# A conditioned decode block: filler matmuls taken out behind the last P.V, four small loads put on another queue, load semaphores shared

## The chip, the cores and the metric

The kernel runs on one core of a Trainium2 chip. The time is the device time of one execution in microseconds (us); before the change it is 665.49, the median of 3 runs (665.31 to 665.92).

## The reference

A decode step for 4 sequences of one token each, in bfloat16: layer norm with conditioned scale and shift, attention over a cache of 4096 positions and 32 heads of width 128, then a gated MLP with its own norm. Cut to what matters:

```python
mod = (silu(c) @ w_mod).reshape(4, 6, 1, 512)      # w_mod 512 x 3072
sa, ca, ga, sb, cb, gb = mod[:, 0], ..., mod[:, 5]
h = layernorm(x) * (1 + ca) + sa
q = (h @ wq) as (B=4, H=32, 1, 128)                # wq 512 x 4096
p = softmax(q . k_cache * 128 ** -0.5)             # k_cache, v_cache: 4 x 32 x 4096 x 128
x = x + ga * ((p . v_cache) as (4, 1, 4096) @ wo)  # wo 4096 x 512
h = layernorm(x) * (1 + cb) + sb
z = gelu(h @ w_in)                                 # w_in 512 x 1792, z1 | z2 of 896 each
g = w_sp * layernorm(z2) + b_sp                    # one token: w_sp and b_sp are scalars
x = x + gb * ((z1 * g) @ w_out)                    # w_out 896 x 512
```

The two caches together are 268 MB and are read once; everything else is some 14 MB.

## The kernel before

**Order and waits.** Every instruction is entered in program order into a list for its engine (`Program.add`, L54). From the tiles that it reads and writes, `Program.depend` (L75) works out which earlier instructions of other engines it must follow, and `Program.order` (L110) which of these need a wait. A wait is for a semaphore that the awaited instruction or load counts up: a load adds 16 to the semaphore that it was given by name (`Program.load`, L164), an instruction 1 to one for its engine and its reader. An engine works through its list strictly in order. The instructions of PE, DVE and ACT that belong to the 15 looped heads stand in a hardware loop of 5 passes with 3 head groups in each; SP, which issues the loads, has them written out. The profile gives DVE and ACT instructions the line of the common helper (L160), matmuls those of `mm` (L382) or `moving` (L392), explicit weight loads L387, and loads L166; so they are told apart by their tiles and their time.

**The front (L410 to L539).** ACT issues four small loads: the 4 rows of c and the 4 rows of x into the tile `rows`, and the scalars w_sp and b_sp into `wb_t`. SP issues w_mod (`wm`, 3 MB), wq (4 MB), then the first K and V (8 MB each). All scratch of the front, `wm`, `wq` and `rows` too, lies in the third of three 8 MB buffers `kv`. PE transposes c and x (eight small matmuls, L506 and L509), ACT and DVE make silu(c), `ln_stats` (L463) makes the mean and the inverse deviation of x by a matmul with a constant matrix, and `mod_part` (L481) makes one of the six modulation vectors with 16 matmuls of 4 columns each; the first two parts read `wm` with a stride of 4 columns. `query` (L493) multiplies by `wq`, once for each sequence, and ACT copies the queries to `qbc`.

**The attention (L624 to L643).** One step is a group of 8 heads of one sequence: 16 steps, of which the last stands outside the loop. In a step, K (8 MB) arrives in one of the three buffers and V in the next. `scores` (L546) multiplies a quarter of K by the query on DVE (the products with 8192 elements for each partition) and adds up over the width on PE with the identity as weights, 16 matmuls of 512 columns; `fold` and `softmax` follow on DVE and ACT; `values` (L594) multiplies by V on PE; `diagonal` (L607) and `project` (L614) pick each head's part and divide by the sum, in the following step. The next K is issued once `diagonal` has freed its buffer (V of the step before).

**The tail (L646 to L770).** Behind the last V, SP issues the late loads into the third buffer (L652 to L656): Wo in three pieces (`GS`), w_in in two (`WJS`), w_out in two (`JFS`); the last four wait until all of V has landed (`v_done`). Each of the seven has a semaphore of its own, `any_late0` to `any_late6`. On PE stand, in order: the last `values`, `sums`, `diagonal` and `project`; `permute` (L661), which puts the heads in the order in which Wo's rows arrive; `output` (L672), 64, 48 and 16 pairs of a weight load and a 4-column matmul (`mm2`, L401), one call for each piece of Wo; the second norm with its statistics matmul; 56 pairs with w_in; two gelus on ACT, with the table for gelu loaded before them (L717) and that for exp and log after (L739); the third norm; 28 pairs with w_out; and a transpose of the result `yo` (L764), a copy and the store.

`busy(n)` (L681) puts fillers between these: it loads the identity as weights and issues n matmuls of 512 columns of `qbc` into a PSUM bank that nobody reads. It is called with 13 before the last P.V and with 2, 2, 5, 2, 2, 7 and 4 behind it.

Of the kernel before, what the change touches and what calls it, by code (L numbers as in the profile page):

```python
# [252 lines left out]
def kernel(  # L253
# [18 lines left out]
    B, _, D = A_x.shape  # L272
    _, H, SK, DH = A_k_cache.shape
# [22 lines left out]
    wb_t = sb.tile([1, 2], BF16, name="wb_t")  # L296
    ident = sb.tile([P, P], BF16, name="ident")
# [19 lines left out]
    qbc = sb.tile([P, NQ, DH], BF16, name="qbc")  # L317
# [10 lines left out]
    def parts(t, a, *ns):  # L328
        for n in ns:
            yield t[:, a:a + n]  # L330
            a += n


    wm, wq, hbc, rows, ones_b, xb, xcT, sg, hn = parts(
        kv[2], 0, J * 6 * D, J * H * DH, J * B * 64, D, P, *(2 * n * J * B for n in (2, 2, 1, 1)),
    )
# [4 lines left out]
    rows, ones_b = rows[0:2 * B], ones_b[0:1]  # L341
# [8 lines left out]
    attn_b, small, po_b, zo_b, s_b = *banks[0:4], banks[4:8]  # L350

    def cut(t, *dims):
        n = 1
        for d in dims:
            n *= d
        t = t[:, 0:n]
        if len(dims) == 1:
            return t
        names = "abcd"[:len(dims)]
        return t.rearrange(  # L360
            f"p ({' '.join(names)}) -> p {' '.join(names)}", **dict(zip(names[1:], dims[1:]))
        )
# [6 lines left out]
    prog = Program(nc, ("PE", "DVE", "ACT"))  # L369

    def dve(name, *args, **kw):
        return prog.call("DVE", name, *args, **kw)
# [13 lines left out]
    def weights(lhsT):  # L386
        prog.add("PE", lambda e, it: e.ldweights(lhsT), [lhsT], [], done=False)  # L387

    def moving(out, lhsT, rhs, start, stop, done=False, sem=None):

        def emit(e, it):
            return e.add_instruction(mybir.InstMatmult(  # L392
                name=nc.get_next_instruction_name(), engine=mybir.EngineType.PE,
                ins=[e.lower_ap(rhs), e.lower_ap(lhsT, for_matmul_weights=True)],
                outs=[e.lower_ap(out)], start_tensor_calc=start, stop_tensor_calc=stop,
                tile_size=(P, P), tile_position=(0, 0), ldweights=False,
                bass_skip_group_check=True,
            ))
        prog.add("PE", emit, [rhs], [out], done=done or sem is not None, sem=sem)
# [7 lines left out]
        return col[:, None, :].to_broadcast([P, n, B])  # L407


    prog.load("ACT", "any_rows_c", rows[0:B], c)  # L410
    prog.load("ACT", "any_rows_x", rows[B:2 * B], A_x.rearrange("b s d -> (b s) d"))
    prog.load("ACT", "any_wb_w", wb_t[:, 0:1], B_w_sp[0:1, 0:1])
    prog.load("ACT", "any_wb_b", wb_t[:, 1:2], B_b_sp.rearrange("(a b) -> a b", b=1))
    tables = "natural_log_exp_and_others"
    prog.add("ACT", lambda e, it: e.preload_act_table_set(tables), [], [], done=False)

    prog.load("SP", "any_wm", wm, w_mod.rearrange("(p j) n -> p (j n)", j=J))
    prog.load("SP", "any_wq", wq, A_wq.rearrange("(p j) n -> p (j n)", j=J))
    wm = wm.rearrange("p (j n) -> p j n", j=J)
    wq = wq.rearrange("p (j g h d) -> p j g h d", j=J, g=G, h=NH)  # L420
# [18 lines left out]
    def load_v(i):  # L439
        n = 2 if i == NQ - 1 else 1  # L440
        w = NT * DH // n
        for a in range(n):
            last = prog.load(
                "SP", f"any_v{a}" if i == NQ - 1 else f"pe_v{i % NB}",
                buf(2 * i + 1)[:, a * w:(a + 1) * w], kv_view(A_v_cache, i)[:, a * w:(a + 1) * w],
            )
        return last
# [143 lines left out]
    def sums():  # L591
        mm(z_ps, mean_d, rsh, True, True, sem="sp")
# [14 lines left out]
    def diagonal():  # L607
        for n in range(4):
            mm(
                o_ps, osb[:, n, :], sel[:, NH * n:NH * n + NH],  # L610
                n == 0, n == 3, sem=("sp", None, None, "dve")[n],
            )

    def project(i):  # L614
        dve("reciprocal", out=rz, in_=z_ps, sem="dve")
        if i >= NQ - 2:
            o = dict(out=oT[:, i + 1])
        else:
            k = (i + 1) % NB
            ov = oT[:, 0:NP * NB].rearrange("p (g k) h -> p g k h", k=NB)  # L620
            o = dict(dyn=lambda g: {"out": ov[:, g, k]})
        dve("tensor_tensor", in0=o_ps, in1=rz, op=MULT, sem="pe", **o)

    load_k(0)  # L624
    for i in range(NQ):
        prog.passno = i // NB if i < NQ - 1 else None
        v_done = load_v(i)
# [23 lines left out]
    GS = [(0, 4), (4, 7), (7, 8)]  # L651
    late = [(wo[:, a:b], wo_v[:, a:b]) for a, b in GS]  # L652
    late += [(win[:, a:b], win_v[:, a:b]) for a, b in WJS]
    late += [(wout[:, a:b], B_w_out[a * P:b * P].rearrange("(p j) n -> p j n", p=P)) for a, b in JFS]
    for n, (t, src) in enumerate(late):
        prog.load("SP", f"any_late{n}", t, src, after=[v_done] if n > 2 else ())  # L656

    oP = oP.rearrange("p (g r b) -> p g r b", g=8, r=4)
    heads = oT[:, 1:].rearrange("p (g b) (e h) -> p h g e b", b=B, e=2)
# [1 line left out]
    def permute(a, b):  # L661
        pp = cut(s_b[2], b - a, 4, B)
        for r in range(4):
            for hl in range(4):
                mm(
                    pp[hl * 32:(hl + 1) * 32, :, r, :], ident[:, r::4],
                    heads[:, hl, a // 2:b // 2], True, True, r == hl == 3,
                    tile_position=(0, hl * 32),
                )
        dve("tensor_copy", out=oP[:, a:b], in_=pp)  # L670

    def output(a, b):  # L672
        for g in range(a, b):
            for r in range(4):
                for jo in range(J):
                    mm2(
                        attn_ps[:, jo, :], wo[:, g, r, jo * P:(jo + 1) * P], oP[:, g, r, :],
                        g == r == jo == 0, g == 7 and r == 3, g == 7 and r == jo == 3,
                    )

    def busy(n, bank=s_b[3]):  # L681

        weights(ident)
        for _ in range(n):
            moving(cut(bank, 4, DH), ident, qbc[:, 0:4, :], True, True)

    busy(13, attn_b)
    permute(0, 6)
    pool("memset", mean_f, 1.0 / FH)
    values(NQ - 1)  # L690
    sums()
    busy(2)
    diagonal()
    project(NQ - 1)
    busy(2)
    permute(6, 8)
    for (a, b), n in zip(GS, (5, 2, 2)):
        output(a, b)
        busy(n)


    x1 = x1b[:, 0]
# [9 lines left out]
    h = h.rearrange("p (j b) -> p j b", b=B)  # L712
    dve("tensor_tensor", out=h, in0=xs, in1=modT[:, 3], op=ADD)

    busy(7)
    gelu = "gelu_apprx_tanh_and_others"
    prog.add("ACT", lambda e, it: e.preload_act_table_set(gelu), [], [], done=False)  # L717
    zp = {1: cut(s_b[0], JF, B), 0: cut(s_b[1], JF, B)}
# [40 lines left out]
    dve("tensor_tensor", out=q, in0=q, in1=bc(rstd, J), op=MULT)  # L759
    yo = yo.rearrange("p (b j) -> p b j", b=B)  # L760
    dve("tensor_tensor", out=yo.rearrange("p b j -> p j b"), in0=q, in1=r1, op=ADD)
    busy(4)
    t_ps = small[0:J * B, 0:P]
    mm(t_ps, yo.rearrange("p b j -> p (b j)"), ident, True, True, True)  # L764
    ot = ot[0:J * B]
# [47 lines left out]
```

## Time and profile before

| | |
|---|---|
| median of 3 runs | 665.49 us (665.31 to 665.92) |
| the profiled execution | 665.31 us, span 663.5 us, mean granted TensorE clock 0.80 |
| busy, share of the span | PE 403.0 us (61%), DVE 391.3 us (59%), ACT 27.3 us, POOL 2.7 us |
| moved | 282.73 MB read, 426 GB/s over the span |
| filler matmuls | 37, 12.3 us busy |
| load from issue to landing | w_mod 10.2 us, wq 20.2 us, the late loads 13.7 to 26.2 us |
| store of the result | 1.4 us from issue to landing |

The span runs from the first to the last instruction; the profiled execution's time has 1.8 us around it. Times inside the span are given as us from its start. A row in order of time reads: start, duration, engine, line, operation, written tile, read tiles, shape, number of merged instructions, and in brackets the engine's idle time before it with what ended that. PEld are weight loads, which overlap with matmuls. A row of merged instructions gives the stretch that they cover. The granted clock is a share of TensorE's full clock.

### The profile page before, as it was taken

What the parts mean: (1) busy time and instruction counts of PE and PEld (TensorE: products, weight loads), DVE (VectorE), ACT (ScalarE), POOL (GpSimd) and SP (SyncE); (2) the same over time, 40 slices, a digit from 0 to 9 for tenths busy, and PEclk for the clock granted to TensorE, in tenths of its full rate; (3) what the DMA queues carried; (4) which work ended last, traced back from release to release, by engine and by line L of the source; (5) the groups of instructions that cost most, each with busy time, mean ns of one, the idle gap of its engine ahead of it and who ended that gap; (6) DMA issues with size and microseconds to landing.
All of it is one profiled execution on the core that took longest, in us unless ns stands there. A gap on an engine that the chain in (4) does not pass through costs nothing.

```text
span 663.5 us, 5137 instructions
## 1 busy us (share of the span) xinstructions
PE 403.0 (61%) x2738; PEld 79.3 (12%) x1749; DVE 391.3 (59%) x331; ACT 27.3 (4%) x64; POOL 2.7 (0%) x11
## 2 busy tenths in 40 slices
PE   2527485563748456374846637494663749466787
PEld 2200101010010101001010100101010010101123
DVE  2058292855829285582928558292855829286942
ACT  1100000000000000000000000000000000000002
POOL 1000000000000000000000000000000000000000
PEclk9959687686968768696876869687686968768996
DMA  9999999999999999999999999999999999999995
GB/s 372 452 435 442 416 431 427 440 435 435 439 431 419 439 442 435 439 431 442 423 423 442 439 435 442 427 431 427 435 442 439 431 435 435 427 427 429 440 407 222
DMA packets 7148, 282.86 MB, mean 426 GB/s; under 512 B 732, under 2 KB 740, under 8 KB 2532
## 3 DMA queue, kind: packets, MB, share of 16 engines
q1 hardware_dynamic: 7120, 282.73, 98.7%
q8 instruction: 7, 0.11, 0.1%
q10 hardware_dynamic: 20, 0.01, 0.0%
q14 instruction: 1, 0.01, 0.0%
HBM read 282.73 MB, written 0.00 MB: 426 GB/s over the span
## 4 chain that ended last, share of the span: by engine, by line
DMA 65%; PE 23%; DVE 11%; issue 0%; SPq 0%; ACT 0%
DMA kv<-in_A_k_cache_dram 58%; PE bank L392 22%; DVE kv L160 11%; DMA kv<-in_A_wo_dram 4%; DMA kv<-in_A_wq_dram 3%; PE bank L382 2%; SPq L166 0%; ACT kv L160 0%; SPq L808 0%; SPq L772 0%
## 5 line engine op out<-in xcount | busy, mean ns | idle before, releaser
L160 DVE TENSOR_TENSOR kv<-kv,qbc 128x8192 bf16<-128x8192 bf16 x64 | 280.3, 4420 | 188.9 <-DMA kv<-in_A_k_cache_dram 188.9
L392 PE MATMUL bank<-kv,ident 128*128 128x512 bf16 x1024 | 261.4, 418 | 159.1 <-DVE kv L160 158.9
L382 PE MATMUL bank<-kv,Ph 128*32 128x512 bf16 x1024 | 88.9, 523 | 1.0 <-DMA kv<-in_A_v_cache_dram 1.0
L160 DVE TENSOR_REDUCE S<-bank 128x64 f32<-128x512 f32 x64 | 43.9, 686 | 36.9 <-PE bank L392 36.9
L382 PE MATMUL bank<-rsh,mean_d 128*128 128x8 f32 x32 | 9.3, 364 | 79.0 <-DVE rsh L160 79.0
L387 PEld LDWEIGHTS <-ident 128*128 128x128 bf16 x72 | 8.7, 121 | 300.4 <-issue 300.4
L160 DVE TENSOR_TENSOR Ph<-E,mask 128x2048 bf16<-128x2048 f32 (+1 forms) x19 | 36.9, 1955 | 10.7 <-ACT E L160 10.7
L382 PEld LDWEIGHTS bank<-kv,Ph 128*32 128x32 bf16 x1024 | 32.9, 127 | 49.5 <-issue 40.7
L160 ACT ACTIVATE E<-S,nm 128x256 f32<-128x256 f32 x16 | 8.1, 508 | 455.1 <-DVE nm L160 455.1
L382 PEld LDWEIGHTS bank<-rsh,mean_d 128*128 128x128 f32 x32 | 7.8, 303 | 140.4 <-DVE rsh L160 140.0
L382 PEld LDWEIGHTS bank<-sel,osb 128*128 128x128 f32 x136 | 17.8, 192 | 55.4 <-issue 54.6
L382 PE MATMUL bank<-sel,osb 128*128 128x8 f32 x136 | 16.3, 247 | 0.0
L160 ACT COPY osb<-bank 128x512 f32<-128x512 f32 x16 | 9.4, 586 | 137.4 <-PE bank L382 137.4
L392 PE MATMUL bank<-qbc,ident 128*128 128x512 bf16 x37 | 12.3, 473 | 0.0
L382 PE MATMUL bank<-kv 128*32 128x512 bf16 x129 | 9.4, 460 | 4.5 <-DMA kv<-in_A_wq_dram 4.5
L387 PEld LDWEIGHTS <-kv 128*128 128x128 bf16 x212 | 6.5, 104 | 5.2 <-DMA kv<-in_A_wo_dram 3.0
L160 DVE TENSOR_REDUCE mx<-S 128x1 f32<-128x256 f32 x16 | 6.7, 420 | 0.5
L392 PE MATMUL bank<-kv,kv 128*128 128x4 bf16 (+1 forms) x212 | 6.5, 168 | 0.6 <-DMA kv<-in_A_wo_dram 0.3
L160 DVE RECIPROCAL rz<-bank 128x8 f32<-128x8 f32 x17 | 3.4, 201 | 4.8 <-PE bank L382 4.8
L382 PE MATMUL bank<-ident,kv 8*128 8x8 bf16 (+2 forms) x9 | 0.6, 176 | 8.4 <-DMA kv<-in_A_x_dram 8.4
L382 PE MATMUL bank<-sT,kv 128*128 128x4 bf16 x96 | 3.7, 169 | 2.4 <-DVE modT L160 1.8
L382 PEld LDWEIGHTS bank<-kv 128*32 128x32 bf16 x129 | 3.9, 114 | 10.0 <-DMA kv<-in_A_wq_dram 4.6
(76 smaller groups left out, 51.4 us busy)
## 6 DMA issues: line engine op xcount, KB each, us to landing
kv<-in_A_k_cache_dram SPq DMA_DIRECT2D x2, 4096.0 KB, 18.9
kv<-in_A_v_cache_dram SPq DMA_DIRECT2D x2, 4096.0 KB, 31.5
kv<-in_A_wq_dram SPq DMA_DIRECT2D x1, 4096.0 KB, 20.2
kv<-in_w_mod_dram SPq DMA_DIRECT2D x1, 3072.0 KB, 10.2
kv<-in_A_wo_dram SPq DMA_DIRECT2D x1, 2048.0 KB, 21.5
kv<-in_A_wo_dram SPq DMA_DIRECT2D x1, 1536.0 KB, 24.8
kv<-in_B_w_in_dram SPq DMA_DIRECT2D x1, 1344.0 KB, 13.7
kv<-in_A_wo_dram SPq DMA_DIRECT2D x1, 512.0 KB, 26.2
```

The lines of the kernel that those rows point to most:

```text
L160: return getattr(e, name)(*args, **kw, **(dyn(it) if dyn else {}))
L382: "PE", lambda e, it: e.matmul(out, lhsT=lhsT, rhs=rhs, start=start, stop=stop, **kw),
L387: prog.add("PE", lambda e, it: e.ldweights(lhsT), [lhsT], [], done=False)
L392: return e.add_instruction(mybir.InstMatmult(name=nc.get_next_instruction_name(), engine=mybir.EngineType.PE, ins=[e.lower_ap(rhs), e.lowe ...
```

## The change

Three things are done.

- The helper `busy` goes, and with it all its calls but the first. The first, 13 matmuls into the bank of the attention's output, is written out in its place. Behind the last P.V, 24 filler matmuls and 7 loads of the identity are gone; the order of the other instructions stays.
- The four small loads (c, x, w_sp, b_sp) are issued by SP in place of ACT, behind w_mod and ahead of wq. ACT's first instruction is now the load of its table.
- The seven late loads count on the semaphores of the loads of w_mod, wq, c, x, the two scalars and the first half of the last K, in place of seven of their own. An early load brings such a semaphore to 16, the late one to 32.

```diff
-    prog.load("ACT", "any_rows_c", rows[0:B], c)
-    prog.load("ACT", "any_rows_x", rows[B:2 * B], A_x.rearrange("b s d -> (b s) d"))
-    prog.load("ACT", "any_wb_w", wb_t[:, 0:1], B_w_sp[0:1, 0:1])
-    prog.load("ACT", "any_wb_b", wb_t[:, 1:2], B_b_sp.rearrange("(a b) -> a b", b=1))
     tables = "natural_log_exp_and_others"
     prog.add("ACT", lambda e, it: e.preload_act_table_set(tables), [], [], done=False)
 
     prog.load("SP", "any_wm", wm, w_mod.rearrange("(p j) n -> p (j n)", j=J))
+    prog.load("SP", "any_c", rows[0:B], c)
+    prog.load("SP", "any_x", rows[B:2 * B], A_x.rearrange("b s d -> (b s) d"))
+    prog.load("SP", "any_w", wb_t[:, 0:1], B_w_sp[0:1, 0:1])
+    prog.load("SP", "any_b", wb_t[:, 1:2], B_b_sp.rearrange("(a b) -> a b", b=1))
     prog.load("SP", "any_wq", wq, A_wq.rearrange("(p j) n -> p (j n)", j=J))
...
+    early = ["any_wm", "any_wq", "any_c", "any_x", "any_w", "any_b", "any_k0"]
     for n, (t, src) in enumerate(late):
-        prog.load("SP", f"any_late{n}", t, src, after=[v_done] if n > 2 else ())
+        prog.load("SP", early[n], t, src, after=[v_done] if n > 2 else ())
...
-    def busy(n, bank=s_b[3]):
-
-        weights(ident)
-        for _ in range(n):
-            moving(cut(bank, 4, DH), ident, qbc[:, 0:4, :], True, True)
-
-    busy(13, attn_b)
+
+    weights(ident)
+    for _ in range(13):
+        moving(cut(attn_b, 4, DH), ident, qbc[:, 0:4, :], True, True)
     permute(0, 6)
     pool("memset", mean_f, 1.0 / FH)
     values(NQ - 1)
     sums()
-    busy(2)
     diagonal()
     project(NQ - 1)
-    busy(2)
     permute(6, 8)
-    for (a, b), n in zip(GS, (5, 2, 2)):
+    for a, b in GS:
         output(a, b)
-        busy(n)
...
-    busy(7)
     gelu = "gelu_apprx_tanh_and_others"
...
     dve("tensor_tensor", out=yo.rearrange("p b j -> p j b"), in0=q, in1=r1, op=ADD)
-    busy(4)
     t_ps = small[0:J * B, 0:P]
     mm(t_ps, yo.rearrange("p b j -> p (b j)"), ident, True, True, True)
```

## The prediction

> **What bounds the kernel.** I read the page's queue table and chain first, then the stages, then the first 42 us and the last 15 us in order of time.
>
> ```profile
> q1 hardware_dynamic: 7120, 282.73, 98.7%
> ...
> DMA 65%; PE 23%; DVE 11%; issue 0%; SPq 0%; ACT 0%
> ```
>
> One load queue holds the 16 DMA engines for 98.7% of the span, and transfers are 65% of the chain that ended last. The stages (us, then busy time and count of PE, PEld, DVE, ACT, POOL; the last three columns are the granted TensorE clock, the DMA share and GB/s):
>
> ```profile
> 60.00:600.00 540.00, 325.26 (x1926) 55.23 (x1091) 332.76 (x236) 16.62 (x42) 0.00 (x0) 0.79 1.00 434
> ...
> 646.00:648.00 2.00, 2.00 (x51) 1.11 (x45) 0.00 (x0) 0.00 (x0) 0.00 (x0) 0.85 1.03 422
> ...
> 652.00:654.00 2.00, 2.00 (x7) 0.53 (x3) 1.19 (x9) 0.20 (x1) 0.00 (x0) 0.50 1.02 416
> 654.00:656.00 2.00, 2.00 (x36) 1.01 (x31) 0.41 (x3) 1.59 (x3) 0.00 (x0) 0.94 0.80 319
> ```
>
> Through the loop the DMA share is 1.00 at 434 GB/s, so the loop runs at the rate of the loads. The clock in the tail is half (0.50) although PE is filled all the time, and comes up again only for the stretch from 654. Now the front, in order of time:
>
> ```profile
> 8.42 0.37 PE L382 MATMUL bank<-ident,kv 8*128 8x8 bf16 x8 [8.42 <-DMA kv<-in_A_x_dram]
> ...
> 12.17 0.70 PE L382 MATMUL bank<-sT,kv 128*128 128x4 bf16 x16 [0.27 <-DVE modT L160]
> ...
> 14.46 0.59 PE L382 MATMUL bank<-sT,kv 128*128 128x4 bf16 x16 [0.74 <-DVE modT L160]
> ...
> 17.45 0.37 DVE L160 TENSOR_SCALAR gwb<-modT,wbf 128x16 f32<-128x16 f32 x2
> 21.68 8.64 PE L382 MATMUL bank<-kv 128*32 128x512 bf16 x116 [4.47 <-DMA kv<-in_A_wq_dram]
> ...
> 41.24 4.42 DVE L160 TENSOR_TENSOR kv<-kv,qbc 128x8192 bf16<-128x8192 bf16 x1 [23.42 <-DMA kv<-in_A_k_cache_dram]
> ```
>
> The work that hangs on c and x runs from 8.42 to 17.82, then PE idles until wq lands and starts the queries at 21.68; the loop's first product waits for K at 41.24. And the tail:
>
> ```profile
> 649.11 1.44 PE L392 MATMUL bank<-kv,kv 128*128 128x4 bf16 x48
> ...
> 651.06 0.68 PEld L387 LDWEIGHTS <-kv 128*128 128x128 bf16 x16 [0.57 <-DMA kv<-in_A_wo_dram]
> 651.21 0.61 PE L392 MATMUL bank<-kv,kv 128*128 128x4 bf16 x16
> ...
> 652.96 2.30 PE L392 MATMUL bank<-qbc,ident 128*128 128x512 bf16 x7
> ...
> 654.66 0.17 DVE L160 TENSOR_TENSOR kv<-xs,modT 128x16 bf16<-128x16 f32 x1
> ...
> 655.10 1.83 PE L392 MATMUL bank<-kv,kv 128*128 128x4 bf16 x56
> ...
> 656.97 0.22 ACT L160 ACTIVATE kv<-bank 128x56 bf16<-128x56 f32 x1 [0.36 <-PE bank L392]
> ...
> 657.20 1.28 ACT L739 ACT_TABLE_LOAD   x1
> ...
> 658.19 1.87 PE L392 MATMUL bank<-qbc,ident 128*128 128x512 bf16 x4
> ...
> 659.34 0.21 DVE L160 TENSOR_TENSOR kv<-q,r 128x16 bf16<-128x16 f32 x1
> ...
> 659.99 0.09 PEld L382 LDWEIGHTS bank<-ident,kv 128*16 128x16 bf16 x1 [1.72 <-DVE kv L160]
> ```
>
> Here the chain is on PE, and fillers (the rows bank<-qbc,ident) stand in it.
>
> **The fillers, place by place.** 24 matmuls and 7 loads of the identity go; the 13 at 633.8 stay. What counts is how long a filler makes PE late for work that was ready.
> - Two at 642.71 (0.22 us each at the full clock): done near 643.15; the next work waits for the copy of osb until 643.18. Nothing.
> - Two at 644.14: done at 644.57; oT is ready at 644.73. Nothing.
> - Five at 647.04: 0.22 us until the clock halves, then 0.43; done near 648.8; the second piece of Wo arrives at about 649.06. Nothing, and every slower matmul before 649 hides behind that arrival too.
> - Two at 650.41: PE reaches the last 16 pairs at 651.21, while their weights were there at 651.02 and the weight load stood at 651.06. 0.14 us late.
> - Two at 651.69: done at 652.49; the squares are ready at 652.45, and the usual gap from DVE to PE is 0.05. Nothing.
> - Seven from 652.96: the 56 pairs with w_in start at 655.10; h is ready at 654.66 + 0.17 = 654.83, so 654.88 was possible (the weights landed at 640.51 + 13.7 = 654.2). 0.22 us late.
> - Four from 658.19: the transpose starts at 659.99; yo is ready at 659.34 + 0.21 = 659.55, so 659.60 was possible. 0.39 us late.
>
> So without fillers the w_in pairs start 0.14 + 0.22 = 0.36 us earlier.
>
> **What the clock takes back.** The seven fillers brought the clock up at 654.2; without them I expect 0.50 to the end. Price of a pair (weight load and 4-column matmul): at full clock 64 of them with Wo take 645.42 to 647.04, 25.3 ns; at half 48 take 649.11 to 650.41, 27.1 ns. The w_in pairs read weights with a stride: (1.83 - 0.17)/55 = 30.2 ns at mostly full clock (0.17: the last one's latency). Strided pairs at half are in the front: in the query stage a group of four 512-column matmuls takes 0.43 us up to 26.27 and 0.21 after it, so PE was at half there before the profile's first clock record (the 1.00 it shows is no record). There 16 strided ones take 0.70 and 16 plain ones 0.59, thus (0.70 - 0.17)/15 = 35 and 28 ns. I take 34 ns for w_in: 55 x (34 - 30.2) = 0.21. Bounds: 0 (the clock comes up anyway), and 55 x 30.2 = 1.66 (every pair doubles); 34 lies by the rows nearest in shape.
> [...]
>
> The second gelu (656.97) thus moves by -0.36 + 0.21 = -0.15. Behind it stand the table load (657.20 to 658.48), Ln, Exp (to 659.03) and the two products up to yo: all -0.15, yo at 659.40. The fp32 statistics matmul of the last norm slows from 0.43 us towards the 0.64 us of the half-clocked one at 652.51; its variance is then ready near 658.1, before the table load ends at 658.33, which hides it. The y pairs wait for wout's second piece, landing near 657.7 (642.70 + 15.0); 12 pairs later is 658.2, no later than now. That landing is what is late next: more than about 0.2 us of further gain on the gelu side would stop at it. The transpose then starts at 659.45 instead of 659.99: **-0.54 us** at the end.
>
> **c, x and the two scalars on the load queue.** Four issues leave ACT (0.56 + 0.26 + 0.27 + 0.27 us there) and stand on SP ahead of wq, K and V: SP's own issues take 0.39 to 0.56, so wq is issued at about 3 instead of 1.39, with K and V behind it. Cover: wm, in flight until 0.94 + 10.2 = 11.1. Without it the queue would idle some 1.6 us. ACT's table load, now at 2.40, comes first; its first user is at 8.72. New wait: c and x land behind wm, near 11.3 in place of 8.3. Queued behind on PE: the eight transposes, the norm, all six modulation parts, and the queries; ACT's exp and the DVE chain follow them. All of it moves by 3.0, ending near 20.8. PE still waits for wq at 21.68, 0.9 us later: 0 on the path. With that cover gone the queries would be late, but the loop's product has qbc by 31.6 and K only at 41.24, another 9.6 us. On the queue, the same four transfers use the same 16 engines as before. Bound: seven transfers in line in the tail (642 to 654) ran at 419 against 434 GB/s, 12 x 15/434 = 0.41 us for about six boundaries, so four cost at most 0.3; from below, 0. I take 0.
>
> **Semaphores.** The late loads count to 32 on semaphores whose first 16 were reached long before (the last, K's first half, landed by 611.3; its partner is issued at 642.7). Same waits, another constant: 0; what hides it is that nothing early is still waiting there.
>
> **Code.** 31 PE instructions less may shift a code fetch: the queue for instructions holds 0.6% of 16 x 20 us between 640 and 660 for two fetches, 0.96 us of one engine each, and the last piece waits for the slowest engine. Taken as 0, bounds -0.6 and +0.6.
>
> Sum: 665.31 - 0.54 = 664.77 for the profiled execution (span 663.5, 1.8 around it). The median is 0.18 above it: **664.95**.
>
> **Rivals.**
> - *The clock turns it (slower).* Place: the 56 and 28 pairs after 654. If halving doubles a pair, the w_in stretch ends at 654.74 + 3.5 = 658.24, 1.31 late; u is ready near 658.8, 28 pairs at 54 ns end near 660.4, and yo comes at 661.3: the transpose 1.36 late, 666.85. It decides once a strided pair costs above about 44 ns (55 x 14 = 0.75 eats 0.36 + 0.39). For: the tail's clock follows the filling. Against: 27.1 beside 25.3 ns.
> - *Small transfers hold their ring (slower).* The output, 4 KB alone, takes 1.4 us from issue to landing; if each of four held the lowest engines so long ahead of wq, their share of every later load ends up to 5.6 late: 670.5. It decides from 0.14 us each. Against: 419 GB/s in the tail.
> - *A code fetch leaves the last loads (faster).* Wo's and w_in's last pieces come up to 0.6 earlier: 664.35, or 663.9 with the clock's upper bound.
> - *The removal does nothing.* The fillers' delays are the shadow of the loads' arrivals: 665.5. Against: yo ready 0.39 us before its reader.
>
> **How the numbers follow.** Forecast 0.60; nothing 0.08; code fetch 0.12; clock 0.11; ring 0.06; something unseen 0.03. By 0.2% (1.33 us, about what a measurement of this kernel tells from no change), slower is the ring, half of the clock case and a little unseen: 0.13. Faster needs 664.16 or less: over half of the code fetch and the edge of the forecast: 0.15. Between them 0.72. The forecast's own range, 664.5 to 665.5, widens downwards by the code fetch to 664.0 and upwards towards the clock case to 666.3.
>
> **What would show it.** Right: the first PE work near 11.3 and the queries still at 21.7; clock 0.50 from 647 to the end; 56 w_in pairs from about 654.75 in some 2.05 us; the transpose 0.05 us after yo; last loads landing within 0.3 us of now. Wrong: w_in pairs over 44 ns, wq or K landing later, a loop above 38.6 us for each head group's K and V, or last loads shifted by more than half a microsecond.

## The result, and the profile after

| | before | after |
|---|---|---|
| median | 665.67 us (12 runs, 665.18 to 666.61) | 664.12 us (12 runs, 663.62 to 665.49) |
| ratio | | 0.9977, 95% interval 0.9968 to 0.9986 |
| profiled execution, span | 665.31, 663.5 | 664.01, 662.1 |

So the kernel is 1.55 us faster by the medians, 0.1 to 0.3% by the interval; 0.54 us had been forecast (664.95). The queue and the chain, from the page after:

```profile
q1 hardware_dynamic: 7140, 282.74, 98.9%
...
DMA 60%; PE 22%; DVE 14%; another core or an unknown queue 2%; issue 1%; ACT 0%; SPq 0%; DVEq 0%
```

The load queue still fills the span, now with the four small loads in it (20 packets more), and the loop still runs at 434 GB/s (60 to 598). Transfers are 60% of the chain in place of 65%; among the rest is one step of 12.19 us from 67.87 that the profile could not assign. The front in order of time (start, duration, engine, line, operation, tiles, count, idle time before):

```profile
11.33 0.37 PE L382 MATMUL bank<-ident,kv 8*128 8x8 bf16 x8 [11.33 <-DMA kv<-in_A_x_dram]
...
20.11 0.37 DVE L160 TENSOR_SCALAR gwb<-modT,wbf 128x16 f32<-128x16 f32 x2
...
20.62 9.35 PE L382 MATMUL bank<-kv 128*32 128x512 bf16 x129 [0.75 <-DMA kv<-in_A_wq_dram]
```

The work on c and x begins 2.91 us later, as SP's order makes it, and ends at 20.48 (20.11 + 0.37), just before wq lets the queries start. The cover was thinner than it had looked: wq landed 1.06 us earlier than in the profile before, so this chain ended 0.14 us ahead of the queries where 0.9 had been counted. Its last rows are not read by the queries; PE itself had been free for 0.75 us (the bracket of the third row), against 4.47 before. It was enough. Now the tail:

```profile
649.21 1.89 PE L392 MATMUL bank<-kv,kv 128*128 128x4 bf16 x64 [1.85 <-DMA kv<-in_A_wo_dram]
651.13 0.17 DVE L160 TENSOR_TENSOR x1b<-bank,modT 128x16 f32<-128x16 f32 x1 [5.70 <-PE bank L392]
...
653.92 0.18 DVE L160 TENSOR_TENSOR kv<-xs,modT 128x16 bf16<-128x16 f32 x1
654.15 1.86 PE L392 MATMUL bank<-kv,kv 128*128 128x4 bf16 x56 [1.74 <-DVE kv L160]
...
656.05 0.22 ACT L160 ACTIVATE kv<-bank 128x56 bf16<-128x56 f32 x1 [0.37 <-PE bank L392]
...
658.42 0.21 DVE L160 TENSOR_TENSOR kv<-q,r 128x16 bf16<-128x16 f32 x1
658.69 0.09 PEld L382 LDWEIGHTS bank<-ident,kv 128*16 128x16 bf16 x1 [1.27 <-DVE kv L160]
```

The reader is to see three things. Wo's second and third pieces are now one unbroken stretch of 64 pairs, where two fillers had parted 48 from 16. The w_in pairs start 0.05 us after h is ready (653.92 + 0.18), and the transpose 0.06 us after yo. And the clock stays down (us, busy time and count of PE, PEld, DVE, ACT, POOL, then granted clock, DMA share, GB/s):

```profile
652.00:654.00 2.00, 0.42 (x2) 0.39 (x3) 1.02 (x7) 0.88 (x3) 0.00 (x0) 0.50 1.04 422
654.00:656.00 2.00, 1.85 (x57) 1.82 (x56) 0.29 (x2) 1.10 (x2) 0.00 (x0) 0.50 0.81 325
```

The 56 w_in pairs take 1.86 us at half clock, against 1.83 at full clock before.

Step by step, profile against profile: the product behind Wo moves from 651.86 to 651.13 (-0.73), h by -0.74, the w_in pairs from 655.10 to 654.15 (-0.95), the second gelu from 656.97 to 656.05 (-0.92), yo from 659.34 to 658.42 (-0.92), the transpose from 659.99 to 658.69 (-1.30), which is the whole difference of the two profiled executions. Two steps fit the forecast (0.22 at the seven, 0.39 at the four); two don't: 0.73 in place of 0.14 at Wo, and 0.03 in place of 0.21 given back to the clock.

Wo's last piece also landed earlier, and that made a second suspect. By the semaphore counts of the trace it came 1.96 us after the second piece before (651.02 and 649.06), and 1.30 after the change (650.46 and 649.16). So 0.56 of the 0.73 us at Wo is the piece itself being there sooner; the later pieces came earlier with it (w_out's second at 656.97 in place of 657.71).

### The profile page after: what moved, and what is told of

The parts are those of the page before. It is cut to its first block, busy times and chain, and to the rows that moved or that the text cites. A ratio compares the mean times of both kernels' runs of the same rounds, so it can differ in the third digit from the quotient of the medians.

```text
span 662.1 us, 5106 instructions
## 1 busy us (share of the span) xinstructions
PE 395.1 (60%) x2714; PEld 79.2 (12%) x1742; DVE 391.3 (59%) x331; ACT 27.3 (4%) x64; POOL 2.7 (0%) x11
## 4 chain that ended last, share of the span: by engine, by line
DMA 60%; PE 22%; DVE 14%; another core or an unknown queue 2%; issue 1%; ACT 0%; SPq 0%; DVEq 0%
DMA kv<-in_A_k_cache_dram 56%; PE bank L392 21%; DVE kv L160 13%; DMA kv<-in_A_wo_dram 4%; PE bank L382 0%; SPq L166 0%; DVE S L160 0%; ACT L733 0%; ACT rstd_ln L160 0%; ACT E L160 0%; DVE x1b L160 0%; DVE mx L160 0%; DVE rsh L160 0%; DVE nm L160 0%
## 5 line engine op out<-in xcount | busy, mean ns | idle before, releaser
L160 DVE TENSOR_TENSOR Ph<-E,mask 128x2048 bf16<-128x2048 f32 (+1 forms) x19 | 36.9, 1955 | 10.7 <-ACT E L160 10.7
```

Of the source, the lines that this page charges most:

```text
L160: return getattr(e, name)(*args, **kw, **(dyn(it) if dyn else {}))
```

## The experiments

All are told against `before` run beside them on the same chip. Ratios are with their 95% interval.

**e1: the fillers alone.** As in the change, `busy` and its calls but the first go; loads and semaphores stay.

```diff
-        busy(n)
...
-    busy(7)
...
-    busy(4)
```

> Only the 24 fillers behind the last P.V are taken out; the small loads stay with ACT and the late loads keep their own semaphores. Theory A (the fillers' delays count 0.14 + 0.22 + 0.39 = 0.75 us, and the other 0.6 us of the gain is earlier landings of the last loads that come with the shorter PE code): the whole gain, 1.3 to 1.6 us below before, Wo's last piece landing near 650.5. Theory B (the 0.6 us of landings comes with the four small loads on SP): 0.7 to 0.8 us below before, the last piece of Wo still near 651.0. Theory C (the 0.6 us is the chance of one execution): 0.7 to 0.8 us in the median, landings scattered.

Measured: 664.10 against 665.58, ratio 0.9978 (0.9967 to 0.9988). The whole gain is the fillers'. Wo's last piece landed 1.29 us after the second.

**e2: the small loads alone.**

```diff
-    prog.load("ACT", "any_rows_c", rows[0:B], c)
...
+    prog.load("SP", "any_c", rows[0:B], c)
```

> Only the four small loads move to SP behind w_mod; fillers and semaphores as before. Theory A: no change in the time (0.1 us either way), last landings as before. Theory B: the last loads land about 0.6 us earlier; the fillers hide part of that (PE is full up to 651.2 and up to 655.1), so 0.2 to 0.6 us below before. The forecast's own term: 0, first PE work near 11.3, queries not later than before.

Measured: 665.78 against 665.58, ratio 1.0001 (0.9992 to 1.0010): no change, as the forecast had it. Theory B falls: here the last piece landed late again, 2.09 us after the second. The tail of this profile held the finding that the later runs followed up:

```profile
652.85 3.17 PE L392 MATMUL bank<-qbc,ident 128*128 128x512 bf16 x7
...
654.55 0.17 DVE L160 TENSOR_TENSOR kv<-xs,modT 128x16 bf16<-128x16 f32 x1
655.81 1.88 PE L392 MATMUL bank<-kv,kv 128*128 128x4 bf16 x56
...
660.37 0.27 PE L382 MATMUL bank<-ident,kv 128*16 128x128 bf16 x1 [0.41 <-DVE kv L160]
```

The PE program is that of before, yet the w_in pairs start 1.09 us after h (654.72), and the transpose 0.05 after yo (660.11 + 0.21). The stages of the same profile show where the clock stood:

```profile
654.00:656.00 2.00, 2.00 (x10) 0.34 (x6) 0.35 (x2) 1.49 (x2) 0.00 (x0) 0.50 0.70 279
656.00:658.00 2.00, 2.00 (x59) 1.92 (x56) 0.21 (x2) 0.45 (x3) 0.00 (x0) 0.90 0.06 25
```

Here the clock came up at about 656.4, behind the seven fillers, so that all of them ran at 0.43 us; before, it came up at 654.2, among them. The same rise is then still there for the four ahead of the transpose, which end in time.

**e3: the semaphores alone.**

```diff
+    early = ["any_wm", "any_wq", "any_rows_c", "any_rows_x", "any_wb_w", "any_wb_b", "any_k0"]
...
-        prog.load("SP", f"any_late{n}", t, src, after=[v_done] if n > 2 else ())
+        prog.load("SP", early[n], t, src, after=[v_done] if n > 2 else ())
```

> Only the late loads count on semaphores of early loads. All theories: no change, within 0.1 us of before. Its profile is a further look at how far the last landings scatter without any change of the work.

Measured: 665.28 against 665.58, ratio 0.9996 (0.9987 to 1.0005). No change that can be told. In its profile the last piece landed 1.87 us after the second.

**e4: only the 13 fillers that stood ahead of ready work.**

```diff
-    for (a, b), n in zip(GS, (5, 2, 2)):
+    for (a, b), n in zip(GS, (5, 0, 2)):
         output(a, b)
-        busy(n)
+        if n:
+            busy(n)
...
-    busy(7)
...
-    busy(4)
```

> Only the fillers that stood ahead of ready work are taken out (2 behind the second piece of Wo, 7 ahead of w_in, 4 ahead of the transpose), 13 of 24; the other 11 stay. By the forecast's place-by-place reading these carry the whole 0.75 us: the same time as with all 24 out (e1), to 0.15 us. If the clock in the tail mattered, the kept ones would make it faster than e1. Rival: the gain goes with the number of instructions, so about 13/24 of e1's.

Measured: 664.12 against 665.58, ratio 0.9975 (0.9965 to 0.9986): the time of e1. Thirteen fillers carry all of it, and which of them lay on the path had been read rightly. What taking them out gains had not: 1.46 by the medians, not 0.75.

**e5: each filler replaced by a load of the identity.** No filler's product was used by anything.

```diff
         for _ in range(n):
-            moving(cut(bank, 4, DH), ident, qbc[:, 0:4, :], True, True)
+            if bank is attn_b:
+                moving(cut(bank, 4, DH), ident, qbc[:, 0:4, :], True, True)
+            else:
+                weights(ident)
```

> Each of the 24 fillers behind the last P.V is replaced, in its place, by one more load of the identity as weights (some 0.05 us each, against 0.22 to 0.43 for a filler): the PE program is as long as before and laid out as before, but the fillers' delays are gone, to 0.1 us. Theory A (the earlier landings come with the shorter PE program, which moves a code fetch to another load engine): Wo's last piece lands 1.9 to 2.1 us after the second, as with the fillers, and the time is 0.75 to 0.95 us below before, 0.5 to 0.7 above e1. Theory D (the fillers' own work on PE holds the last loads back): the piece lands 1.3 us after the second, as in e1, and the time is that of e1, some 1.5 below before. Theory E (the fillers' delays were mis-sized, the landings are a side show): the time of e1 whatever the landings.

Measured: 664.23 against 665.86, ratio 0.9974 (0.9965 to 0.9983), and the last piece 1.29 us after the second. From its profile:

```profile
649.44 2.01 PE L392 MATMUL bank<-kv,kv 128*128 128x4 bf16 x64 [1.89 <-DMA kv<-in_A_wo_dram]
...
652.36 0.62 PEld L387 LDWEIGHTS <-ident 128*128 128x128 bf16 x8
...
654.27 0.17 DVE L160 TENSOR_TENSOR kv<-xs,modT 128x16 bf16<-128x16 f32 x1
654.50 1.86 PE L392 MATMUL bank<-kv,kv 128*128 128x4 bf16 x56 [1.74 <-DVE kv L160]
```

The program is as long as before and the gain is there in full: the length and layout of the PE program are not its cause, and theory A falls. What is gone is the time that fillers held PE. The early landing came along in this run too, so it does not part theory D from theory E.

**e6: fillers out, PE's code padded in the front.** The 31 loads write nothing.

```diff
+    for _ in range(31):
+        weights(ident)
     for b in range(B):
```

> The fillers are out as in e1, and 31 loads of the identity are put in the front ahead of the queries, where PE waits for wq: the PE program has its old length, with nothing added to the tail. Theory A by length: the landings as before (1.9 to 2.1 us from Wo's second to its last piece), 0.5 to 0.7 us above e1. Theory A by place in the tail, D and E: landings and time of e1, 1.5 us below before. None expects a change in the front, since the loads there wait for nothing that PE does.

Measured: 664.24 against 665.86, ratio 0.9975 (0.9964 to 0.9985), the last piece 1.49 us after the second. The time of e1 again.

**e7: the other 13 fillers out, those ahead of the last P.V.**

```diff
-    busy(13, attn_b)
```

> The other way about: the 24 fillers behind the last P.V stay, and the 13 ahead of it go (14 PE instructions). Theory A: Wo's last piece lands 1.3 us after the second, as without the fillers, and PE, held by its two fillers, gains at most 0.3 us from that; the clock may halve earlier, which slows the last P.V by up to 1.5 us behind the arrival of Wo (none on the path). Theory D: 1.9 to 2.1 us, as before. For the seven fillers ahead of w_in this is a further look: they end 0.1 to 1.1 us after h is ready, by where the clock comes up.

Measured: 665.47 against 665.86, ratio 0.9993 (0.9984 to 1.0003): no change that can be told. Here the last piece landed early, 1.31 us after the second, with the 24 fillers in place, so theory D doesn't hold as a rule, and nothing was gained by the landing: the two fillers held PE, and the 16 pairs started 2.06 us after the 48. The seven held the w_in pairs by 1.05 us.

**e8 and e9: the gain in two halves.** e8 takes out only the two between Wo's pieces, e9 only the seven and the four.

```diff
 # e8
-    for (a, b), n in zip(GS, (5, 2, 2)):
+    for (a, b), n in zip(GS, (5, 0, 2)):
 # e9
-    busy(7)
-    busy(4)
```

> Only the two fillers between Wo's second and last piece go; 22 stay. Forecast's sizes: 0.14 us below before. Revised theory (the two hold the last 16 pairs to some 2.1 us after the start of the 48; without them PE follows the landing at some 1.3 us): the 16 pairs start 1.3 to 1.4 us after the start of the 48 and the time is 0.6 to 0.75 us below before, less or more by where the clock comes up among the seven.

> Only the seven ahead of w_in and the four ahead of the transpose go; the two stay. Forecast's sizes: 0.61 us below before, less the clock's 0.21, so 0.4. Revised theory: 0.5 to 1.05 us by where the clock would have come up, less 0.03 for the slower clock, so some 0.8 us below before; e8 and e9 together make up e4's 1.46.

Measured: e8 665.40 against 665.57, ratio 0.9993 (0.9984 to 1.0002); e9 664.76 against 665.57, ratio 0.9991 (0.9981 to 1.0000). Neither interval excludes no change, and e8's is wide enough for either size; its median (0.17) is at the forecast's 0.14, not at the revised 0.6 to 0.75. The halves add up to 0.98 us by the medians, less than e4's 1.46. e8's profile (an execution of 668.19, whose loads came some 1.6 us later) shows one way for that: the 16 pairs follow at 1.3 us as expected, but the clock never comes up in its tail, and the seven (1.05 late) and the four (0.40) both cost their full price. In it the five fillers behind Wo's first piece, counted as nothing, were not harmless either, since the work ahead of them came some 3 us later:

```profile
649.84 2.29 PE L392 MATMUL bank<-qbc,ident 128*128 128x512 bf16 x5
...
651.92 1.89 PE L392 MATMUL bank<-kv,kv 128*128 128x4 bf16 x64
```

The second piece had landed at 650.70, 1.2 us before its pairs started. Whether any of this holds for the other executions of e8, all at least 1.4 us shorter, wasn't seen.

**e10: twice the seven.** All other fillers behind the last P.V are out.

```diff
-    busy(7)
+    busy(14)
```

> All other fillers behind the last P.V are out, and 14 instead of 7 stand ahead of w_in. Forecast's reading (the clock is up at the fourth of them): the w_in pairs start about 1.7 us after h, 1.7 us above e1, 0.2 above before. Revised theory (the rise stands at a boundary of 3.41 us windows that run free of the kernel): they start 1.9 to 3.1 us after h, so 0.4 to 1.6 above before, and the end of the 14 follows the profile's clock records to 0.1 us at 0.427 us each before the rise and 0.216 after it.

Measured: 667.75 against 665.57, ratio 1.0029 (1.0017 to 1.0040): slower by 1.9 us by the ratio (1.1 to 2.7), where the forecast's reading gave 0.2 and the revised theory 0.4 to 1.6. From the profile, first in order of time, then by stage:

```profile
652.74 5.45 PE L392 MATMUL bank<-qbc,ident 128*128 128x512 bf16 x14
...
654.43 0.17 DVE L160 TENSOR_TENSOR kv<-xs,modT 128x16 bf16<-128x16 f32 x1
658.02 1.83 PE L392 MATMUL bank<-kv,kv 128*128 128x4 bf16 x56
```

```profile
656.00:657.00 1.00, 1.00 (x4) 0.00 (x0) 0.00 (x0) 0.00 (x0) 0.00 (x0) 0.50 0.18 72
657.00:658.00 1.00, 1.00 (x5) 0.11 (x1) 0.00 (x0) 0.00 (x0) 0.00 (x0) 0.84 0.01 3
```

The clock's record puts the rise at 657.32, 4.58 us after the first of the fourteen: 4.58/0.427 = 10.7 of them at half, 3.3 x 0.216 = 0.71 us for the rest, end at 658.03; the pairs start at 658.02. The rule for their end holds to 0.01 us. The pairs start 3.42 us after h (654.43 + 0.17), more than the expected 1.9 to 3.1, since the rise came 4.58 us after the first filler, later than in any other profile (1.1 to 3.7 where there was one).

**e11: the 11 fillers out that the forecast held harmless.**

```diff
-    busy(2)
...
-    for (a, b), n in zip(GS, (5, 2, 2)):
+    for (a, b), n in zip(GS, (0, 2, 0)):
```

> The counterpart of e4: only the 11 fillers go that stood where PE waited anyway (2 + 2 ahead of Wo's first piece, 5 behind it, 2 behind the last); the other 13 stay in front of ready work. Forecast and revised theory: no change by what they delay (0.1 us), though a later or missing rise of the clock among the seven can add up to 0.8 us. A gain that goes with the number of instructions would be 11/24 of 1.5, some 0.7 us below before. The 16 pairs start some 2.1 us after the start of the 48 again.

Measured: 666.04 against 665.69, ratio 1.0007 (0.9998 to 1.0016): no gain, so the gain doesn't go with the number of instructions. Its profile has the two fillers and an early landing, by which the price of the two can be read:

```profile
650.09 0.10 PEld L387 LDWEIGHTS <-ident 128*128 128x128 bf16 x1
...
650.92 0.61 PE L392 MATMUL bank<-kv,kv 128*128 128x4 bf16 x16
```

The last piece had landed at 650.05; PE loaded the identity and ran its two fillers, and took up the 16 pairs 0.87 us later, 0.83 more than the usual 0.04.

## Why the sign was right and the size too small

The measured 664.12 lies below the forecast's own range, 664.5 to 665.5, and just inside the wider one, whose lower edge of 664.0 stood for the code fetch. So it was covered by the allowance for a rival, not by the working.

Right: the front costs nothing (e2), the semaphores cost nothing (e3), the removal counts, in the medians, only where a filler stands ahead of ready work (e4 against e11), and those three places are the ones named. The rival with the small transfers holding their ring is refuted by e2. The clock rival failed on its price: it needed 44 ns for a strided pair, and they take (1.86 - 0.17)/55 = 30.7 at half clock (1.86 to 1.91 us for the 56 in the seven profiles that ran them at half throughout).

Wrong are three sizes and the fixed landings, all taken from one execution:

| profile with these fillers | last piece after second | two hold Wo's last 16 pairs by | seven hold w_in by | four hold the transpose by | sum |
|---|---|---|---|---|---|
| before | 1.96 | 0.15 | 0.22 | 0.39 | 0.76 |
| e3 | 1.87 | 0.25 | 0.12 | 0.39 | 0.76 |
| e2 | 2.09 | 0.09 | 1.04 | 0.00 | 1.13 |
| e7 | 1.31 | 0.76 | 1.05 | 0.01 | 1.82 |
| e11 | 1.29 | 0.83 | 1.05 | 0.00 | 1.88 |

Each entry is the start of the work less the time when it could have started in that same execution: its last input plus the usual 0.04 to 0.05 us.

- "Two at 650.41 ... 0.14 us late" set the end of the fillers against a landing that scatters from execution to execution. Wo's last 16 pairs started 2.06 to 2.13 us after the start of the 48 in every profile with the two, wherever the piece landed. In the seven profiles with the two out or replaced it landed 1.27 to 1.49 us after the second, and in the change PE took it up without a break. So the two fillers cost up to 0.83 us when the piece is early. The step of 0.73 between the two profiles that were compared is 0.15 of holding and 0.56 of an earlier landing (0.02 is left).
- "Seven from 652.96 ... 0.22 us late" and "Four ... 0.39" hang on where the clock rises. If it rises some 1.3 or 1.1 us into the seven (before, e3), they cost 0.61 and 0.51 together; if it rises behind them (e2, e7, e11), 1.04 to 1.06.
- "55 x (34 - 30.2) = 0.21" for the clock took the price of strided pairs from the front, where 16 stand alone; in a run of 56 it is 0.03.
- "Taken as 0" for the code, and "That landing is what is late next": the forecast held the last loads where they were, and a shift of more than half a microsecond was one of its own signs of being wrong. Wo's last piece came 0.56 and w_out's second 0.74 us earlier. That mattered: in the profile after, the y pairs end at 657.50 (656.54 + 0.96) and ACT's part of yo's input at 658.11. With w_out still at 657.71 the y pairs would have ended near 658.2 and yo, by an estimate from the rows before, some 0.5 us later than it did. In e4 yo's chain did wait for that piece: it landed at 657.15, and the sum that hangs on the y pairs ended at 658.20, behind ACT's at 658.17.

The mean of the five sums is 1.27; e1, e4, e5 and e6 gained 1.46 to 1.63 by their medians, and their intervals (gains of 0.12 to 0.36%, 0.8 to 2.4 us) hold both. What the fillers held is shown; whether the gain is that alone, or in part landings that come earlier without them, the medians don't tell. The forecast's working gives 0.76 for the profile of before, as low as any of the five: it was worked out on an execution in which the fillers happened to be cheap. The profiled 665.31 lies below the later median of 665.67, a small sign of it.

The rival with the code fetch named the right landing (0.6 us earlier) and nearly the right time (664.35). Its other figure, 663.9, doesn't follow from its terms: 664.35 - 0.21 is 664.14. The shorter program is not the reason: e5 has the old length and the early landing. What places that landing early or late stays open. It was late in 4 of the 6 profiles with the two fillers and in none of the seven without, while e7 and e11 show that it can be early with them.

The semaphore counts narrow it down. A piece adds 16 counts as its parts land. In the four late profiles (before, e2, e3, e9) fifteen counts of Wo's last piece are there and the sixteenth follows 0.58 to 0.80 us later; for the second piece that gap was 0.04 to 0.13. In the nine others the gap grows by no more than 0.05 from one piece to the next. In all thirteen one code fetch (a load of instructions, queue q8) of 16 KB, 0.88 us long, starts between 0.73 us before and 0.81 us behind the second piece's landing. A fetch that holds up the part which is last anyway would make a late landing, and one that holds up a part well ahead would not; the profile doesn't say which engine took it, so this is argued, not shown.

No version here beats the change: e1, e4, e5 and e6 are all within 0.15 us of it by the medians.

## What to carry to other kernels

A filler stands in line ahead of real work: it costs whatever is left of it when that work is ready, and its time follows the clock that it is itself meant to raise, 0.22 us or 0.43 each here. Before one is kept for the clock's sake, measure the work behind it at both clocks; here strided pairs with 4 columns cost 30.2 and 30.7 ns, and there was next to nothing to win. And a delay that hangs on two things which both moved between executions, here the landing of a load (1.27 to 2.10 us behind the one before) and the rise of the clock (1.1 to 4.6 us behind the first filler ahead of w_in, or none), is a distribution: read it from several profiles, or give it the whole range. The same holds for the landings that a forecast takes as fixed.

## What was unexpected of the hardware

- In the profile of before, which holds 64 clock records, each starts one to ten steps of 3.41 us behind the one ahead of it, to 0.04 us (654.23 to 657.64 is one step); so it is with the 62 of the profile after. Against the kernel this grid lay elsewhere in other executions: before, the clock changed in the tail at 647.40, 654.23 and 657.64 (two steps and one); in e2 at 646.15, 656.39 and 659.80 (three and one), though the tail's work stood at nearly the same times (the 48 pairs of Wo's second piece at 649.11 and 648.97).
- A PE that the profile shows as full did not by that bring the clock up: in e8, 650 to 658 has PE busy for 2.00 of every 2.00 us at 0.50. Fillers are some 5.7 of these 8 us. Counted by the grid, from 0.43 us for each filler at half clock, the clock came up in the tail at the end of every step of 3.41 us in which fillers held PE for 2.3 us or more (e3 2.3, before 2.5, e7 2.7, e2 2.8, e11 3.0, e10 3.4), and of none in which they held it for 2.1 or less (e8: 2.1, 2.0, 1.8). In these rows the rise goes with where the grid cuts the seven fillers; no run was made to find what is counted. After the change PE's waits in the tail are 1.85 us at most, and the clock is half from 646.24 to the end.
- Loading the identity in place of a filler took 0.06 to 0.09 us each in e5 (6 in 0.34 us, 8 in 0.62, 3 in 0.26).
- Wo's last piece, 0.5 MB, landed 1.27 to 2.10 us behind the piece ahead of it in the thirteen profiles, whose late loads are the same.
